# A linear-attention and mixture-of-experts kernel: the first own table and its gathers a step sooner, the second weight matrix loaded in the middle of the loop, other work moved between engines

## The chip, the cores and the metric

One core of one Trainium2 chip runs the whole program. The metric is the device time of one execution in microseconds (us); the kernel before took 648.4 us, the median of three runs (647.74 to 648.51).

## What is computed

A linear attention with decay gives `x`, 3072 rows of 512, and a layer of 8 experts with two experts per row follows. Cut from the reference:

```python
# attention, 4 batches, 8 heads, 768 positions, 64 wide, one decay gamma per head
state = gamma * state + einsum(k[t], v[t]);  y[t] = scale * einsum(q[t], state)
x = y.transpose(0, 2, 1, 3).reshape(3072, 512)
# experts
logits = x @ w_gate;  noisy = logits + log1p(exp(x @ w_noise)) * noise
top2 = two largest of noisy per row;  top2_w = softmax over the two
for e in range(8):  out[rows of e] += top2_w * (relu(x[rows of e] @ w1[e]) @ w2[e])
```

## The kernel before

**Stages.** The attention runs as a loop of 24 steps (`for j in range(NCH)`), one chunk of 128 positions each, 6 chunks per batch, from about 4 to 107 us. Behind the loop the first expert (number 0) begins, while the last chunk is still being routed; the eight experts then fill the rest of the span. All engines work through their instructions in the order in which the program writes them.

**One step j of the loop**, in the order written: `qk(j+1)` (TensorE, into PSUM tile `pA`), `x_turn(j-1)` (TensorE turns the scaled output `yt` back into rows and computes the gate products, into `pT`, of which there is one buffer), `y_state(j)` (TensorE, needs the state `U`), the entries of `middle` (TensorE pieces of the routing), `v_scale(j+1)` (GpSimd, gives `vp`), `masked(j+1)` twice (VectorE, frees `pA`), `x_scale(j-1)` (ScalarE squares `pT` and VectorE makes a power of two of the sum), the loads of chunk j+4 and the store of chunk j-2 on SyncE's DMA queue, `x_split(j-1)` (ScalarE reads `pT` at L411 and L425, makes the f16 high part at L426, and GpSimd the low part at L427), `y_mm(j)` (TensorE L373, then VectorE's `yt` at L377, then TensorE's state update L383 and ScalarE's copy `U` at L385), and last the entries that `P` (`mid`), `at` (`todo`) and `at0` (`first_todo`) have put into this step. So the VectorE entries of step j run while TensorE is already in step j+1.

**HALVES.** `x_turn(j)` uses 16 matmuls for a chunk in `HALVES` (even chunks below 16) and 32 half as wide ones for the others.

**Routing.** Chunks 0 to 11 are routing group 0, 12 to 17 group 1, 18 to 23 group 2: `route_x`, `route_b`, `route_t`, `route_i`, `route_m` (VectorE, with an Exp and an Ln on ScalarE), `route_p` (TensorE counts), `route_n`, `route_g` (gates), `route_d`. `gates_out` writes the gates to `xbuf` in HBM. For expert 0 the rows of group 0 are listed by `own_a`, `own_h`, `own_t`, `own_m`, `own_s`, `slots`; the first three blocks of 128 rows are then fetched by `gather` (GpSimd, an indirect DMA from `xbuf`) in steps 18 to 20 and turned by `x_t` (a DMA transpose on SyncE's queue, into `xe`) in steps 20 and 21.

**Weights.** `w_load` brings a quarter of a matrix (512 KB), `w_sum` squares it (ScalarE L210), `w_scale` (TensorE L220, VectorE) makes the scale, `w_hi` and `w_lo_half` the two f16 parts. w1 of expert 0 is loaded in steps 3 to 6, w2 in steps 20 and 21.

**Behind the loop**, in the order written: `gates_out(1)`, `route_d(1)`, `first(0)` (12 matmuls, L880 to L882, need `xe` of the first three blocks), `w_sum` of w2's last two quarters, four zero fills of the output, `x_store(22)`, `x_turn(23)`, `logits(23)`, `route_x(2)`, `x_scale(23)`, `x_last(23)`, `first(1)` with `w_scale` of w2 after its first six matmuls, `route_b/t/i/m(2)`, `first(2)`, `first(3)` with `route_p(2)` (L498, L500) after its first six matmuls, and so on.

Of the kernel before, what the change touches and what calls it, by code (L numbers as in the profile page):

```python
# [10 lines left out]
F32 = mybir.dt.float32  # L11
F16 = mybir.dt.float16
# [3 lines left out]
AF = mybir.ActivationFunctionType  # L16
OP = mybir.AluOpType
# [4 lines left out]
NC = S // C  # L22
NCH = B * NC
N = B * S
DM = H * D
# [35 lines left out]
SOON = _C["vtab"][1]  # L61
QW = HP * C + NC * HP
WARM, BUSY = (5, 2), 3
HALVES = range(0, 16, 2)


def _constants():
# [37 lines left out]
def moe_kernel(ctx, tc, qk_rows, vk_rows, noise, wgn, w1, w2, ctab, qtab, xbuf, out):  # L105
# [158 lines left out]
    def load(j, pairs=("qk", "vk")):  # L264
        for n in pairs:
            t = loads.tile([128, 2, DM], F32, name="in_" + n, bufs=AHEAD + 1)
            nc.sync.dma_start(t.rearrange("p a c -> p (a c)"), {"qk": qk_rows, "vk": vk_rows}[n][j])
            if n == "qk":
                IN["q", j], IN["k", j] = [t[:, i].rearrange("p (a c) -> p a c", a=HP) for i in range(2)]
            else:  # L270
                IN["v", j], IN["kt", j] = t[:, 0], t[:, 1]
# [47 lines left out]
        u = loads.tile([128, HP, D], F32, name=f"U{i}", bufs=1)  # L319
        U.append(u)  # L320

    VP, AM, PY, PT, YT, XS, X16, LG = {}, {}, {}, {}, {}, {}, {}, {}
    pctx = ExitStack()
    loop_psum = pctx.enter_context(tc.tile_pool(name="loop_psum", bufs=1, space=bass.MemoryType.PSUM))
    pU = psum.tile([128, 512], F32, name="pU")[:, :HP * 64].rearrange("p (a d) -> p a d", a=HP)
# [93 lines left out]
        nc.vector.tensor_scalar(XS[j].bitcast(I32), m[:, :1], -1.0, float((127 + TX + 62) << 23), op0=OP.mult, op1=OP.add)  # L419

    def x_split(j):
        X16[j] = x = work.tile([128, 2, DM], F16, name="x16", bufs=3)
        x32 = loads.tile([128, DM], F32, name="x32", bufs=2)
        logits(j)
        nc.scalar.activation(x32.rearrange("p (n x) -> p n x", x=64), PT.pop((j, "y")), AF.Copy, scale=XS[j])  # L425
        nc.scalar.activation(x[:, 0], x32, AF.Copy)  # L426
        nc.gpsimd.tensor_tensor(x[:, 1], x32, x[:, 0], op=OP.subtract)  # L427

    def x_last(j):
        X16[j] = x = work.tile([128, 2, DM], F16, name="x16", bufs=3)  # L430
# [87 lines left out]
        nc.vector.reciprocal(dn, dn)  # L518
        R[g] = (t2, den, dn)

    def route_g(g):

        t2, den, dn = R[g]
        sl, n = span(g), SPAN[g][1]
        nc.vector.tensor_tensor(ga[:, 0, sl], dn, invx[:, sl], op=OP.mult)
        nc.vector.tensor_tensor(ga[:, 1, sl], den, ga[:, 0, sl], op=OP.mult)
        t = temp([128, 2, n, NL], F32, "t", n)
        nc.vector.tensor_tensor(t, oh[:, :, sl], ga[:, :, sl, None].to_broadcast([128, 2, n, NL]), op=OP.mult)
        nc.vector.tensor_tensor(gateb[:, sl], t[:, 0], t[:, 1], op=OP.add)
        if g:  # L530
            nc.gpsimd.tensor_copy(gateb[:, sl, 0:1], gateb[:, sl, E:NL])

# [181 lines left out]
    def at(j, f, *a):  # L714
        todo.setdefault(j, []).append((f, a))
# [35 lines left out]
    def at0(j, f, *a):  # L751
        first_todo.setdefault(j, []).append((f, a))
# [3 lines left out]
    def P(j, f, *a, d=mid):  # L756
        d.setdefault(j, []).append((f, a))
# [5 lines left out]
    at0(12, route_x, 0, 6, 12)  # L763
    P(13, route_b, 0, 6, 12)
    P(13, route_t, 0, 6, 12)
    P(13, route_i, 0, 6, 8)
    P(14, route_i, 0, 8, 12)
    P(14, route_m, 0)
    at0(14, route_c, 0)
    P(15, route_p, 0, d=middle)  # L770
    P(15, route_n, 0)
    P(15, route_g, 0)
    P(16, route_d, 0)
    at(16, gates_out, 0)
    P(16, own_a, 0)
    P(16, own_h, 0, 0, 7)
    at(16, route_e, 0)
    P(17, own_h, 0, 7, 12)
    P(17, own_t, 0)
    P(18, own_m, 0, 0, 2 * NC, d=middle)  # L780
    P(18, own_s, 0)
    P(18, slots, 0, 3)
    for t in range(3):
        at(18 + t, gather, 0, t)
    P(20, x_t, 0, 0)
    P(21, x_t, 0, 1)
    at(21, x_t, 0, 2)
    at0(18, route_x, 1, 0, 6)
    P(20, route_b, 1, 0, 6)
    P(20, route_t, 1, 0, 6)  # L790
    P(21, route_i, 1, 0, 6)
    P(22, route_m, 1)
    at0(22, route_c, 1)
    P(23, route_p, 1, d=middle)
    P(23, route_n, 1)
    P(23, route_g, 1)
    at(3, turn_ident, 1)
    at(3, turn_gate, 1)
    at(1, nc.vector.memset, zero, 0.0)
    for i in range(4):  # L800
        at(3 + i, w_load, 0, "1", i)
        at0(5 + i, w_sum, 0, "1", i)
        at0((9, 9, 10, 11)[i], w_hi, 0, "1", i)
        at((20, 20, 21, 21)[i], w_load, 0, "2", i)
        if i < 2:
            at0(22 + i, w_sum, 0, "2", i)
    first_todo[9].insert(0, (w_scale, (0, "1")))
    for i, j in ((0, 10), (2, 10), (4, 11), (6, 12), (1, 18), (3, 19), (5, 19), (7, 21)):
        P(j, w_lo_half, 0, "1", i)
    at(3, nc.sync.dma_start, nz.rearrange("p c e -> p (c e)"), noise)  # L810
    at(4, nc.sync.dma_start, ct, ctab[:, SOON:])
# [16 lines left out]
    for j in range(NCH):  # L828
        more = j + 1 < NCH
        pA = qk(j + 1) if more else None  # L830
        if j:
            x_turn(j - 1)
        y_state(j)
        for f, a in middle.get(j, []):
            f(*a)
        if more:
            v_scale(j + 1)
        if more:
            masked(j + 1, pA, 0)
            masked(j + 1, pA, 1)  # L840
        if j:
            x_scale(j - 1)
        if j < NC - 3:
            q_table(j + 3)
        if j + AHEAD < NCH:
            load(j + AHEAD)
        if j > 1:
            x_store(j - 2)
        if j:
            x_split(j - 1)  # L850
        if j == 0:
            turn_gate(0)
        y_mm(j)
        for f, a in mid.get(j, []) + todo.get(j, []):
            f(*a)
        for f, a in first_todo.get(j, []):
            f(*a)
# [145 lines left out]
        return mm1_pe(0, 0, FIRST, f, between)  # L1003

    j = NCH - 1
    gates_out(1)
    route_d(1)
    p0 = first(0)
    for i in range(2, 4):
        w_sum(0, "2", i)  # L1010
    for i in range(4):
        zero_out(i)
    x_store(j - 1)
# [278 lines left out]
```

## Time and profile before

| what | value |
|---|---|
| median of three runs | 648.4 us |
| the profiled execution, its own time | 650.09 us |
| its span | 648.3 us |
| mean granted TensorE clock, as a share of full speed | 0.996 |
| TensorE matmul busy | 626.4 us (97%) |
| VectorE / ScalarE / GpSimd busy | 292.4 / 304.1 / 202.3 us |
| DMA | 113.05 MB, mean 174 GB/s |

A busy share is an average over stages. TensorE is the engine that is nearly always busy, so what counts is where it is not, what ends these waits, and where its steps in the loop are longer than the matmuls alone ask for.

### The profile page before, as it was taken

The numbers are of one execution on the slowest core, as the hardware profiler recorded it, in microseconds if no ns is written. First come the engines' busy times: TensorE is split into PE (matmuls) and PEld (weight loads), VectorE is DVE, ScalarE is ACT, GpSimd is POOL, SyncE is SP. The second block draws the span as 40 slices with busy tenths as digits, with TensorE's granted clock in tenths as the row PEclk, the third lists the DMA queues.
The fourth block names the chain that finished last, engine by engine and source line by source line (L and its number), as shares of the span: only waits on it lengthen the run. The fifth ranks groups of instructions, "written<-read, shape, count | busy, mean of one in ns | idle before, by whom it ended". The sixth has DMA issues, their size and how long they took to land.

```text
span 648.3 us, 12929 instructions
## 1 busy us (share of the span) xinstructions
PE 626.4 (97%) x5271; PEld 379.3 (59%) x5271; DVE 292.4 (45%) x743; ACT 304.1 (47%) x582; POOL 202.3 (31%) x165
## 2 busy tenths in 40 slices
PE   8999997799999999999999999999999999999995
PEld 5888885448668644554455445544554465445574
DVE  4677995698445222635163216321632172215020
ACT  5778455713653543443454345534553454344121
POOL 2545574031431044104330342034303430340214
PEclk9999998999999999999999999999999999999999
DMA  8999979998679066744775476547774775572303
GB/s 319 407 403 400 314 254 190 363 250 283 146 131 301 10 113 125 199 140 88 127 189 168 82 121 177 187 83 119 188 175 83 111 205 159 83 131 50 50 8 44
DMA packets 87513, 113.05 MB, mean 174 GB/s; under 512 B 59894, under 2 KB 61052, under 8 KB 83868
## 3 DMA queue, kind: packets, MB, share of 16 engines
q1 hardware_dynamic: 75664, 85.56, 43.7%
q0 software_dynamic: 11776, 26.63, 22.0%
q8 instruction: 42, 0.69, 0.4%
q14 instruction: 19, 0.16, 0.1%
q10 hardware_dynamic: 12, 0.01, 0.0%
HBM read 72.66 MB, written 26.42 MB: 153 GB/s over the span
## 4 chain that ended last, share of the span: by engine, by line
PE 87%; DVE 5%; DMA 3%; ACT 2%; issue 1%; POOL 1%; SPq 1%; POOLq 0%; ACTq 0%; DVEq 0%
PE pH L880 13%; PE pH L881 13%; PE pH L882 13%; PE pO L926 11%; PE pO L928 11%; PE pO L927 11%; PE pY L373 3%; PE pT L982 2%; PE pA L349 2%; PE pO L970 2%; PE pT L400 2%; DMA xg<-xbuf,idx 2%; DMA in_vk<-vk 1%; PE pY L366 1%; DMA wst<-w 1%
## 5 line engine op out<-in xcount | busy, mean ns | idle before, releaser
L880 PE MATMUL pH<-xe,w1h 128*128 128x384 f16 (+5 forms) x576 | 181.6, 315 | 3.5 <-DMA xe<-xg 2.8
L917 POOL DMA_INDIRECT out<-ot,idx x51 | 81.9, 1606 | 322.7 <-ACT ot L912 181.7
L881 PE MATMUL pH<-xe,w1h 128*128 128x384 f16 (+5 forms) x576 | 181.6, 315 | 0.0
L882 PE MATMUL pH<-xe,w1l 128*128 128x384 f16 (+5 forms) x576 | 181.5, 315 | 0.0
L889 DVE SCALAR_TENSOR_TENSOR hl<-pH,hh 128x384 f16<-128x384 f32 (+5 forms) x144 | 75.6, 527 | 139.8 <-ACT hh L886 139.1
L928 PE MATMUL pO<-w2h,hl 128*128 128x512 f16 x344 | 130.4, 379 | 0.0
L927 PE MATMUL pO<-w2l,hh 128*128 128x512 f16 x344 | 130.4, 379 | 0.0
L926 PE MATMUL pO<-w2h,hh 128*128 128x512 f16 x344 | 130.4, 379 | 0.0
L886 ACT ACTIVATE hh<-pH 128x384 f16<-128x384 f32 (+5 forms) x144 | 67.2, 468 | 122.6 <-PE pH L882 111.7
L912 ACT ACTIVATE ot<-pO,gse 128x512 f32<-128x512 f32 x45 | 30.9, 687 | 155.2 <-PE pO L928 142.9
L238 DVE SCALAR_TENSOR_TENSOR w1l<-wst,wsc,w1h 128x1024 f16<-128x1024 f32 x28 | 35.9, 1283 | 97.4 <-ACT w1h L233 97.4
L880 PEld LDWEIGHTS <-w1h 128*128 128x128 f16 x576 | 56.5, 98 | 37.4 <-issue 4.3
L882 PEld LDWEIGHTS <-w1l 128*128 128x128 f16 x576 | 56.5, 98 | 31.3 <-issue 0.5
L881 PEld LDWEIGHTS <-w1h 128*128 128x128 f16 x576 | 56.5, 98 | 31.0 <-issue 1.5
L210 ACT ACTIVATE junk<-wst 128x1024 bf16<-128x1024 f32 x64 | 67.2, 1050 | 4.9 <-DMA wst<-w 4.9
L729 POOL DMA_INDIRECT xg<-xbuf,idx x54 | 56.9, 1053 | 28.0 <-issue 13.3
L928 PEld LDWEIGHTS <-hl 128*128 128x128 f16 x344 | 33.7, 98 | 40.6
L926 PEld LDWEIGHTS <-hh 128*128 128x128 f16 x344 | 33.7, 98 | 40.5 <-issue 0.4
L927 PEld LDWEIGHTS <-hh 128*128 128x128 f16 x344 | 33.7, 98 | 39.6
L427 POOL TENSOR_TENSOR x<-x,x 128x512 f16<-128x512 f32 x23 | 28.7, 1249 | 40.5 <-ACT x L426 14.4
L233 ACT ACTIVATE w2h<-wst,wsc 128x1024 f16<-128x1024 f32 x32 | 36.5, 1140 | 0.6 <-DVE wsc L188 0.6
L233 ACT ACTIVATE w1h<-wst,wsc 128x1024 f16<-128x1024 f32 x32 | 36.1, 1137 | 0.0
(182 smaller groups left out, 656.1 us busy)
## 6 DMA issues: line engine op xcount, KB each, us to landing
wst<-w SPq DMA_DIRECT2D x28, 1024.0 KB, 5.3
in_qk<-qk SPq DMA_DIRECT2D x24, 512.0 KB, 5.2
in_vk<-vk SPq DMA_DIRECT2D x24, 512.0 KB, 7.8
xbuf<-x SPq DMA_DIRECT2D x24, 256.0 KB, 5.2
out<-zero SPq DMA_DIRECT2D x6, 1024.0 KB
wst<-w SPq DMA_DIRECT2D x8, 512.0 KB, 7.3
xg<-xbuf,idx POOLq DMA_INDIRECT x54, 4.4
xe<-xg SPq DMA_TRANSPOSE x54, 4.6
```

Of the source, the lines that this page charges most:

```text
L210: nc.scalar.activation(junk, st[:, i * 1024:(i + 1) * 1024], AF.Square, accum_out=ss[:, i:i + 1])
L233: nc.scalar.activation(hi, st[:, i * 1024:(i + 1) * 1024], AF.Copy, scale=sc[:, 0:1])
L729: nc.gpsimd.indirect_dma_start(out=x[:n], out_offset=None, in_=xbuf[:128 + B0 * S] if e == 0 and t < 3 else xbuf, in_offset=bass.IndirectO ...
L880: nc.tensor.matmul(p[:, :n], whi, xh, start=(k == 0), stop=False)
L881: nc.tensor.matmul(p[:, :n], whi, xl, start=False, stop=False)
L882: nc.tensor.matmul(p[:, :n], wlo, xh, start=False, stop=(k == KT - 1))
L886: nc.scalar.activation(hh[:, f, n0:n1], p, AF.Relu)
L889: nc.vector.scalar_tensor_tensor(hl[:, f, n0:n1], p, 0.0, hh[:, f, n0:n1], op0=OP.max, op1=OP.subtract)
L917: nc.gpsimd.indirect_dma_start(out=out, out_offset=bass.IndirectOffsetOnAxis(ap=idx[:n, i:i + 1], axis=0), in_=ot[:n], in_offset=None, com ...
L926: nc.tensor.matmul(p, a, WT["2h"][:, f, :], start=(f == 0), stop=False)
L927: nc.tensor.matmul(p, a, WT["2l"][:, f, :], start=False, stop=False)
L928: nc.tensor.matmul(p, c, WT["2h"][:, f, :], start=False, stop=(f == FT - 1))
```

## The change

The own table of expert 0 is made about a step earlier: all of `route_i(0)` in step 13, `route_d` and `own_a` in step 15, `own_h` in 15 and 16, `own_t` in 16, `own_m`, `own_s`, `slots` in 17; the gathers go to steps 17 to 19 and the transposes, each an entry of `mid` now, to 19 to 21. The two larger instructions of `route_g` (L528, L529) run on GpSimd for groups 0 and 1. Group 1's steps move one step forward, and `gates_out(1)` and `route_d(1)` go into steps 22 and 23. w2 of expert 0 is loaded in steps 14 to 17, one quarter each, and squared in steps 18, 20 and 22 and behind the loop. w1 is loaded from step 2 on, its `w_hi` goes to steps 10 to 13, one each, and its `w_lo_half` is spread anew. For chunks 0 to 5 and 8 (`DIRECT`) ScalarE writes the f16 high part straight from PSUM and VectorE makes the low part, from PSUM too; that low part, or for other chunks L426 and L427, now stands behind `y_mm`, so that the copy of `U` comes before them. `HALVES` gets 18, 20 and 22. The first load of v and k is two DMAs.

```diff
-HALVES = range(0, 16, 2)
+HALVES = [*range(0, 16, 2), 18, 20, 22]
+DIRECT = [0, 1, 2, 3, 4, 5, 8]
...
+            if n == "vk" and j == 0:
+                for i in range(2):
+                    nc.sync.dma_start(t[:, i], src[:, i * DM:(i + 1) * DM])
...
     def x_split(j):
-        x32 = loads.tile([128, DM], F32, name="x32", bufs=2)
+        X16[j] = work.tile([128, 2, DM], F16, name="x16", bufs=3), PT.pop((j, "y"))
         logits(j)
-        nc.scalar.activation(x32.rearrange("p (n x) -> p n x", x=64), PT.pop((j, "y")), AF.Copy, scale=XS[j])
-        nc.scalar.activation(x[:, 0], x32, AF.Copy)
-        nc.gpsimd.tensor_tensor(x[:, 1], x32, x[:, 0], op=OP.subtract)
+        x, py = X16[j]
+        if j in DIRECT:
+            nc.scalar.activation(x[:, 0].rearrange("p (n x) -> p n x", x=64), py, AF.Copy, scale=XS[j])
+        else:
+            X32[0] = loads.tile([128, DM], F32, name="x32", bufs=2)
+            nc.scalar.activation(X32[0].rearrange("p (n x) -> p n x", x=64), py, AF.Copy, scale=XS[j])
+
+    def x_low(j):
+        x, py = X16[j]
+        X16[j] = x
+        if j in DIRECT:
+            xv = [x[:, a].rearrange("p (n x) -> p n x", x=64) for a in range(2)]
+            nc.vector.scalar_tensor_tensor(xv[1], py, XS[j], xv[0], op0=OP.mult, op1=OP.subtract)
+        else:
+            nc.scalar.activation(x[:, 0], X32[0], AF.Copy)
+            nc.gpsimd.tensor_tensor(x[:, 1], X32[0], x[:, 0], op=OP.subtract)
...
-    def route_g(g):
+    def route_g(g, eng=nc.vector):
...
-        nc.vector.tensor_tensor(t, oh[:, :, sl], ga[:, :, sl, None].to_broadcast([128, 2, n, NL]), op=OP.mult)
-        nc.vector.tensor_tensor(gateb[:, sl], t[:, 0], t[:, 1], op=OP.add)
+        eng.tensor_tensor(t, oh[:, :, sl], ga[:, :, sl, None].to_broadcast([128, 2, n, NL]), op=OP.mult)
+        eng.tensor_tensor(gateb[:, sl], t[:, 0], t[:, 1], op=OP.add)
...
-    P(13, route_i, 0, 6, 8)
-    P(14, route_i, 0, 8, 12)
+    P(13, route_i, 0, 6, 12)
...
-    P(15, route_g, 0)
-    P(16, route_d, 0)
+    P(15, route_d, 0)
+    P(15, own_a, 0)
+    P(15, route_g, 0, nc.gpsimd)
+    P(15, own_h, 0, 0, 2)
     at(16, gates_out, 0)
-    P(16, own_a, 0)
-    P(16, own_h, 0, 0, 7)
-    at(16, route_e, 0)
-    P(17, own_h, 0, 7, 12)
-    P(17, own_t, 0)
-    P(18, own_m, 0, 0, 2 * NC, d=middle)
-    P(18, own_s, 0)
-    P(18, slots, 0, 3)
+    P(16, own_h, 0, 2, 12)
+    P(16, own_t, 0)
+    P(16, route_e, 0)
+    P(17, own_m, 0, 0, 2 * NC, d=middle)
+    P(17, own_s, 0)
+    P(17, slots, 0, 3)
     for t in range(3):
-        at(18 + t, gather, 0, t)
-    P(20, x_t, 0, 0)
-    P(21, x_t, 0, 1)
-    at(21, x_t, 0, 2)
+        at(17 + t, gather, 0, t)
+        P(19 + t, x_t, 0, t)
...
     for i in range(4):
-        at(3 + i, w_load, 0, "1", i)
-        at0(5 + i, w_sum, 0, "1", i)
-        at0((9, 9, 10, 11)[i], w_hi, 0, "1", i)
-        at((20, 20, 21, 21)[i], w_load, 0, "2", i)
-        if i < 2:
-            at0(22 + i, w_sum, 0, "2", i)
-    first_todo[9].insert(0, (w_scale, (0, "1")))
-    for i, j in ((0, 10), (2, 10), (4, 11), (6, 12), (1, 18), (3, 19), (5, 19), (7, 21)):
+        at(2 + i, w_load, 0, "1", i)
+        at0((5, 6, 8, 9)[i], w_sum, 0, "1", i)
+        at0(10 + i, w_hi, 0, "1", i)
+        at(14 + i, w_load, 0, "2", i)
+        if i < 3:
+            at0((18, 20, 22)[i], w_sum, 0, "2", i)
+    first_todo[10].insert(0, (w_scale, (0, "1")))
+    for i, j in ((0, 11), (1, 11), (2, 12), (3, 12), (4, 14), (5, 18), (6, 18), (7, 20)):
...
         y_mm(j)
+        if j:
+            x_low(j - 1)
...
-    gates_out(1)
-    route_d(1)
     p0 = first(0)
-    for i in range(2, 4):
-        w_sum(0, "2", i)
+    w_sum(0, "2", 3)
```

## Rows read from the trace of the kernel before

**Rows 1.** Windows: us, then each engine's busy time, granted clock, DMA share, GB/s.

```profile
11.42:27.00 15.58, 15.58 (x358) 14.22 (x354) 11.18 (x27) 10.75 (x31) 8.61 (x8) 1.00 1.03 409
...
72.73:89.44 16.71, 15.86 (x368) 13.64 (x365) 16.02 (x44) 8.64 (x23) 10.09 (x8) 1.00 0.87 285
89.44:107.20 17.76, 15.59 (x361) 13.06 (x359) 13.16 (x48) 11.70 (x31) 11.26 (x11) 1.00 0.92 195
107.20:123.24 16.04, 9.86 (x78) 5.22 (x77) 7.32 (x45) 8.57 (x19) 1.40 (x2) 0.89 0.93 302
123.24:160.00 36.76, 36.76 (x280) 23.64 (x280) 34.24 (x92) 11.04 (x21) 7.99 (x7) 1.00 0.87 270
```

**Rows 2.** Timeline of TensorE behind the loop: start, us, what, idle before and releaser.

```profile
109.98 0.40 PE L880 MATMUL pH<-xe,w1h 128*128 128x384 f16 x1 [2.77 <-DMA xe<-xg]
...
113.71 0.78 PE L400 MATMUL pT<-turn,yt 64*64 64x80 f32 x32
...
116.58 0.16 PE L220 MATMUL pR<-wsb,oneb 128*128 128x4 bf16 x1 [1.01 <-ACT wsb L216]
...
119.37 0.33 PE L882 MATMUL pH<-xe,w1l 128*128 128x384 f16 x1
...
123.24 0.18 PE L498 MATMUL pR<-mb,trib 128*128 128x54 bf16 x1 [1.65 <-DVE mb L487]
```

**Rows 3.** First gather (timeline), last gather (chain), the transposes that wait (timeline).

```profile
88.44 1.15 POOL L729 DMA_INDIRECT xg<-xbuf,idx  x1 [0.17 <-issue]
...
96.78 10.14 DMA xg<-xbuf,idx
...
97.56 11.09 SPq L747 DMA_TRANSPOSE xe<-xg  x2
```

**Rows 4.** Timeline of ScalarE behind the loop.

```profile
113.51 1.06 ACT L210 ACTIVATE junk<-wst 128x1024 bf16<-128x1024 f32 x1 [4.37 <-DMA wst<-w]
...
116.44 0.21 ACT L411 ACTIVATE lgs<-pT 128x64 f32<-128x64 f32 x1
```

**Rows 5.** Timeline of the loop's first step: GpSimd's first v_scale, TensorE's first y_mm.

```profile
8.84 1.04 POOL L330 TENSOR_TENSOR vp<-in_vk,cs 128x512 f32<-128x512 f32 x1 [7.77 <-DMA in_vk<-vk]
...
9.93 1.09 PE L373 MATMUL pY<-am,vp 128*64 128x128 f32 x16 [1.23 <-POOL vp L330]
```

**Rows 6.** Chain that ended last, undisturbed steps: start, us on the chain, what.

```profile
19.25 1.09 PE pA L349 x16
...
22.82 0.47 PE pU L383 x16
23.28 1.09 PE pA L349 x16
...
27.01 1.09 PE pA L349 x16
```

**Rows 7.** Timeline of TensorE: four waits inside the loop.

```profile
42.71 0.49 PE L373 MATMUL pY<-am,vp 128*64 128x128 f32 x5 [0.59 <-issue]
...
70.70 0.21 PE L498 MATMUL pR<-mb,trib 128*128 128x108 bf16 x1 [0.72 <-DVE mb L487]
...
76.86 1.75 PE L349 MATMUL pA<-in_qk 64*128 64x128 f32 x16 [0.33 <-DVE am L354]
...
104.70 0.71 PE L400 MATMUL pT<-turn,yt 64*64 64x80 f32 x28 [1.13 <-issue]
```

**Rows 8.** Timeline: VectorE's route_g, own_h, low part in x_last; the gates' DMA and landing.

```profile
73.94 1.23 DVE L528 TENSOR_TENSOR t<-oh,ga 128x216 f32<-128x216 f32 x1
...
82.48 0.82 DVE L571 TENSOR_TENSOR a<-lanes,lf 128x640 f16<-128x640 f16 x1
...
119.64 0.75 DVE L434 SCALAR_TENSOR_TENSOR x<-pT,xsa,x 128x512 f16<-128x512 f32 x1 [0.81 <-ACT x L433]
...
76.23 0.39 SPq L536 DMA_DIRECT2D xbuf<-gateb  x1
...
DMA to landing us min/median/max: 3.0/3.0/3.0
```

## What I predict

> **What bounds the kernel now.** I read the windows first, then TensorE's timeline behind the loop, then who ends its waits there, and last its waits inside the loop. The windows [rows 1] show three kinds of stretch. From 123.24 on TensorE is busy all the time (36.76 of 36.76 us), so whatever reaches that point sooner makes the end sooner by as much, as long as everything that follows moves with it. From 107.20 (the end of the last `y_mm`) to 123.24 it is busy for 9.86 of 16.04 us, and its granted clock is 0.89 of full speed: this is the gap. Inside the loop it is nearly always busy; an undisturbed step takes 4.03 us with the 16-matmul `x_turn` and 3.73 with the 32-matmul one, from one `qk` to the next [rows 6], and the later steps are longer. VectorE, 16.02 of 16.71 us busy between 72.73 and 89.44, is what TensorE waits for there.
>
> The gap has four parts [rows 2]. `first(0)` waits 2.77 us for `xe`. Its 12 matmuls then take 3.73 us (109.98 to 113.71), while 17 such matmuls behind the second wait take 2.79 (116.58 to 119.37), so 12 would take 1.95: after the wait they run at the lower of the two clock levels, 1.2 GHz. `w_scale` of w2 costs 1.01, `first(3)` then waits for `x_last`, and `route_p(2)` waits 1.65 for the routing of the last chunk. The releasers lead back to one place. The last gather took 10.14 us to land, beside the loads of w2, and the transposes on SyncE's queue waited for it (11.09 us with the two issues) [rows 3]; the second half of w2 stands behind them in that queue, so ScalarE waits 4.37 us for it, and `logits(23)`, behind the two sums in ScalarE's order, starts at 116.44 although its `x_turn` was done at 114.49 [rows 2, 4].
>
> **The change part by part. Behind the loop.** Gathers and transposes come a step sooner, without w2 in their way. A step is some 4 us, so the last gather goes out about 92.5; even if it took its 10.14 us again, it would be there at 102.6, before the loop's end. So I take the wait at 0, and the lower clock with it. What is late next: `first(0)` takes 1.95 us, `x_turn(23)` 0.78, and from `logits(23)` to `route_p(2)` the path takes 123.24 - 116.44 = 6.80 us, the way through `x_scale`, `x_last`, `route_b` to `route_m`, which the change leaves alone; its TensorE work in between (first(1), first(2), half of first(3), 4.9 us) is hidden by it. That gives 9.5 us. The other end: `w_sum` of the last quarter still stands before `logits(23)`, and the sum in step 22 is in front of it on ScalarE; with about 1.25 us each (1.06 [rows 4] and the readout, estimated) ScalarE can be up to 1 us late, so 10.5. I take 10.0, the middle, since ScalarE's two sums fall where it also makes the high part. 16.04 - 10.0 = **6.0 saved** (5.5 to 6.5). `gates_out(1)` and `route_d(1)` leave this place for steps where VectorE has little else; I count nothing for them, and under 0.5 if that cover fails.
>
> **v and k apart.** The first `y_mm` waits 1.23 us for `vp`, and that for the load [rows 5]. At 409 GB/s [rows 1] the 256 KB of k are 0.6 us. `qk(1)` lies in front of it on TensorE and leaves room. **0.6 saved** (0 if the halves land together, to 0.65).
>
> **The low part by VectorE.** In the seven steps behind the chunks in `DIRECT`, 0.75 us [rows 8] comes behind `yt` on VectorE, and the next `x_turn` now waits for it, since it reads the only `pT`. `yt` (estimated at 0.7 from the low part, which has its size) and the low part end some 1.65 us after `y_mm`, with a hop of about 0.1 each; TensorE has 0.47 + 1.09 = 1.56 us of its own in between [rows 6]. So the least is 0.1 a step, 0.7 in all; where VectorE is late anyway (it is 72% busy there, 11.18 of 15.58 [rows 1]) it is the whole 0.75, 5.3 in all. Near the lower end, with one late step and the chunk behind which TensorE has no `pU` to make, I take **1.5 lost**. The copy of `U` in front of the high part, and GpSimd's work that falls away, save nothing on TensorE there. `w_hi` one to a step instead of two takes a peak off ScalarE; I count nothing for it.
>
> **Steps 14 to 18.** Four `route_i` leave step 14, so `route_m` comes sooner and the 0.72 wait of `route_p(0)` can go; `route_g`'s 1.23 and its smaller companion leave VectorE [rows 8], and with them the 0.33 wait of `qk` at 76.86 and its stretch to 1.75 [rows 7] instead of 1.09 [rows 6]. That is 1.7 of gain. Against it, `own_h` for ten chunks and `own_t` now stand just before `own_m` of the next step: five chunks took 0.82 [rows 8], so with `own_t` some 2 us behind `yt`, about what TensorE has to do until `own_m`; if VectorE is a little late, TensorE waits up to 1. **1.0 saved** (0 to 1.7), nearer the gain, since the heavier of VectorE's instructions leave.
>
> A rule weighs on this. L528 took 1.23 us for 216 columns and the low part 0.75 for 512 [rows 8]: the row is long for its size. The Trainium skill, GPSIMD Engine Reference, section 8 (Key points), says that GpSimd shares its SBUF interfaces with VectorE, that instructions with two SBUF inputs contend, and that VectorE is about twice as fast at elementwise work. By that rule the move to GpSimd makes the work longer and holds up `own_a` and `own_h` beside it, and this part's 1.0 would be 0; the row shows the contention before the move already, so I keep 1.0.
>
> **Steps 19 to 23.** The wait of 1.13 us at 104.70 names no engine [rows 7]; it falls when w2 and the gather fill the DMA engines, which the change ends, so 1.1 saved (0 to 1.13). 18, 20 and 22 in `HALVES` cost 4.03 - 3.73 = 0.3 a step [rows 6], 0.9 lost (0 where the step waits for VectorE anyway). The sums of w2 in steps 18 and 20 put 1.25 us in front of ScalarE's next square, and `x_turn` waits for `pT` behind it: 0.4 lost (0 to 2.5). Group 1's entries come a step sooner, and the last step of the loop holds none of the heavy ones: 1.0 saved (0 to 2, since TensorE stands idle for 17.76 - 15.59 = 2.2 us there [rows 1], 1.1 of them counted already, and is slowed besides). **0.8 saved** (-2.3 to 3.1).
>
> **w2 in the loop.** Four loads of 512 KB are 2.1 MB, 5.1 us at 409 GB/s, in a stretch whose DMA share is 0.87 [rows 1]. The inputs are asked for three steps, some 12 us, ahead, so I see no wait for them. The nearest cost is the nameless wait of 0.59 at 42.71 [rows 7], from a stretch where w1 was just loaded; none to two such: **0.5 lost** (0 to 1.2).
>
> **The sum**: 6.0 + 0.6 - 1.5 + 1.0 + 0.8 - 0.5 = 6.4 us. The profiled execution took 650.09 us with a span of 648.3; it would be 643.7 and 641.9. The median of the runs, 648.4, lies at the span, so the forecast is 648.4 - 6.4 = **642.0**. Its own range is 640 to 644.5.
>
> **The rivals.** (a) *The loop gives back all that it waits for*: the low part hides wholly (0.7 lost), steps 14 to 23 give 1.7 + 2.5 and w2 costs nothing: 6.2 + 0.6 - 0.7 + 4.2 = 10.3, 638.1. For it speaks VectorE's load, against it that the change puts ScalarE's sums into the same steps. (b) *`xe` is late all the same*: gates or gathers are held up by w2's transfers, and `first(0)` still waits 1 to 2 us and then runs at the lower clock (1.8 more); of 6.4 some 3 remain, 645.3. For it speaks that the loads of w2 now end just where the gathers begin; against it the 4 us of room. (c) *Slower: the first gather blocks GpSimd.* It reads the gates that `gates_out(0)` writes, and behind it in GpSimd's order stands the `v_scale` of a chunk whose `y_mm` comes about a step later. The gates went out at 76.23 and landed in 3.0 us [rows 8]; the first gather was issued at 88.44 [rows 3], now at about 84. If the gates stand behind all of w2 (5.1 us), they land at about 85 and cost next to nothing. From about 87 on, when that `y_mm` is due, each further us is a us lost; beyond 93.4, 17 us after the issue, all 6.4 are gone, and at 96 the time is 651.0. For it speaks that the gates are 1536 short rows, against it the landing of 3.0 us in a loaded stretch. The Trainium skill, DMA: Bandwidth & Descriptors, Specifications, wants pieces of 512 bytes or more for full rate; no row here shows the gates' rate by itself. (d) *Nothing gained*: `DIRECT` costs its 5.3 and ScalarE's sums their 2.5: 6.4 - 3.8 - 2.1 = 0.5 left, 647.9.
>
> **How the numbers follow.** Chances: the forecast 0.62, (a) 0.12, (b) 0.14, (c) 0.07, (d) 0.05. The range takes in the forecast's own, (b) and half of (a): **638.0 to 646.0**. About 0.2% (1.3 us) is what a measurement of this kernel can tell from no change; forecast, (a) and (b) lie beyond that: faster 0.88, same 0.05, slower 0.07.
>
> **What would show it.** In the profile after: `first(0)` starts right behind the last `y_mm`, without a wait on `xe`, at a granted clock of 1.00 (if not, (b)); w2's last sum ends before or about when `x_turn(23)` does, `logits(23)` follows at once, and `route_p(2)` still waits for `mb`, with about 10.0 us from the loop's end to it. The loop's end lies at 106 to 107.5. `x_turn` in the first steps waits for L434's like on VectorE by 0.1 to 0.75. GpSimd's gather in step 17 does not hold its `v_scale` (if it does, (c)). The forecast is wrong if TensorE shows new idle time behind `route_p(2)`, where I moved everything together, or if the chain from `logits(23)` to `mb` is no longer 6.8 us.

## The result: slower by 1.2%

The changed kernel took 655.86 us, median of four runs (655.11 to 656.24); the kernel before took 648.43 beside it. The ratio is 1.0116, 95% interval 1.0098 to 1.0133. The prediction was 642.0, faster; it was wrong in sign. The profiled execution took 656.14 us, with a span of 654.3 and a mean granted clock of 0.990. The profiled execution of the kernel before (650.09) was 1.7 above its median, so the two traces show 6.0 of the 7.4 us between the medians.

The windows of the changed kernel (us, busy time of each engine, granted clock, DMA share, GB/s): an early stretch, one in the loop, the part behind the loop, the stretch after it up to 160 us.

```profile
11.42:27.00 15.58, 14.58 (x324) 12.98 (x320) 11.63 (x28) 7.97 (x25) 5.74 (x6) 1.00 1.02 407
...
93.58:108.18 14.60, 11.02 (x182) 9.68 (x178) 11.35 (x27) 6.71 (x17) 8.92 (x8) 0.78 0.81 279
...
119.56:129.21 9.65, 7.94 (x76) 4.61 (x76) 5.21 (x36) 6.83 (x15) 1.33 (x2) 1.00 0.88 312
129.21:160.00 30.79, 30.79 (x214) 18.21 (x214) 28.98 (x81) 9.08 (x16) 8.37 (x7) 1.00 0.87 253
```

Against [rows 1]: the part behind the loop is 9.65 us where it was 16.04, and from 129.21 on TensorE is busy all the time, as it was before from 123.24 on. But the loop ends at 119.56 instead of 107.20, and TensorE, which had no idle time in the early stretch, now has 1.0 us there. The timeline around the loop's end (start, us, what, idle before and releaser):

```profile
111.06 1.29 SPq L765 DMA_TRANSPOSE xe<-xg  x1
...
119.50 0.34 PE L899 MATMUL pH<-xe,w1h 128*128 128x384 f16 x1
...
121.55 0.78 PE L406 MATMUL pT<-turn,yt 64*64 64x80 f32 x32
...
122.40 0.23 ACT L417 ACTIVATE lgs<-pT 128x64 f32<-128x64 f32 x1 [0.20 <-PE pT L406]
...
129.21 0.18 PE L516 MATMUL pR<-mb,trib 128*128 128x54 bf16 x1 [1.65 <-DVE mb L505]
```

Beside [rows 2 to 4]: `first(0)` starts with no wait, the last transpose takes 1.29 where two took 11.09, and from `logits(23)` to `route_p(2)` it is 6.81 us as it was 6.80. So the part behind the loop gained and the whole loss lies in the loop. This table gives it in stretches, each from one `qk` to another on TensorE's timeline, each row from one profiled execution (`qk(k)` is the first TensorE work of step k - 1; LE is the end of the last `y_mm`; us):

| kernel | to qk(8) | 8 to 13 | 13 to 16 | 16 to 20 | 20 to 22 | 22 to LE | LE to `route_p(2)` | sum |
|---|---|---|---|---|---|---|---|---|
| before | 34.5 | 21.5 | 11.4 | 18.3 | 8.7 | 12.8 | 16.0 | 123.2 |
| changed | 37.4 | 21.4 | 16.6 | 18.2 | 14.6 | 11.3 | 9.7 | 129.2 |
| changed, halves apart | 37.2 | 21.3 | 12.8 | 18.2 | 9.5 | 11.4 | 9.7 | 120.1 |
| changed, halves from PSUM | 37.1 | 21.6 | 15.2 | 18.2 | 9.5 | 11.3 | 9.7 | 122.6 |
| changed, old w1 schedule | 36.4 | 21.5 | 11.2 | 18.2 | 12.7 | 12.0 | 9.7 | 121.7 |
| changed, old low part | 35.2 | 21.2 | 16.2 | 18.6 | 14.5 | 11.4 | 9.7 | 126.7 |
| changed, both | 34.5 | 21.7 | 12.9 | 18.2 | 10.1 | 14.0 | 9.7 | 121.1 |
| changed, w2 late | 36.2 | 21.7 | 14.9 | 19.8 | 8.7 | 11.3 | 11.7 | 124.4 |
| before, w2 early | 34.5 | 21.5 | 11.4 | 18.2 | 10.0 | 11.7 | 10.0 | 117.3 |
| before, new w1 schedule | 34.2 | 21.3 | 16.9 | 17.4 | 11.0 | 13.3 | 14.4 | 128.5 |

The changed kernel loses 2.9 us before qk(8), 5.2 from qk(13) to qk(16) and 5.9 from qk(20) to qk(22). Two lines of the list of what ends TensorE's waits in the loop (us in total, times, longest); between them stand smaller waits for ScalarE and waits that name no engine:

```profile
PE pA L355 <- DVE am L360: 4.4, 3, 2.7
...
PE pT L406 <- DVE x L442: 1.6, 4, 0.6
```

The last line is the low part in the early steps. The first is `masked`, VectorE's work that frees `pA`. What made it late is in the timeline of VectorE and GpSimd in steps 11 and 12, then in step 18:

```profile
59.22 1.17 POOL L445 TENSOR_TENSOR x<-x,x 128x512 f16<-128x512 f32 x1 [1.50 <-DMA in_vk<-vk]
59.50 2.88 DVE L246 SCALAR_TENSOR_TENSOR w1l<-wst,wsc,w1h 128x512 f16<-128x512 f32 x2
60.33 1.50 POOL L336 TENSOR_TENSOR vp<-in_vk,cs 128x512 f32<-128x512 f32 x1
62.30 1.28 DVE L360 TENSOR_TENSOR am<-pA,mask 128x512 f32<-128x512 f32 x2
...
65.48 1.29 POOL L445 TENSOR_TENSOR x<-x,x 128x512 f16<-128x512 f32 x1 [3.64 <-DMA in_qk<-qk]
65.66 1.31 DVE L465 TENSOR_TENSOR lgs<-lgs 128x192 f32<-128x192 f32 x1
66.72 1.15 POOL L336 TENSOR_TENSOR vp<-in_vk,cs 128x512 f32<-128x512 f32 x1
67.01 0.98 DVE L466 TENSOR_TENSOR lg<-lgs 128x96 f32<-128x96 f32 x1
...
71.36 1.34 PE L406 MATMUL pT<-turn,yt 64*64 64x80 f32 x32 [0.96 <-ACT x L435]
...
93.33 1.15 POOL L747 DMA_INDIRECT xg<-xbuf,idx  x1 [0.17 <-DVE xsa L425]
93.86 3.83 DVE L246 SCALAR_TENSOR_TENSOR w1l<-wst,wsc,w1h 128x512 f16<-128x512 f32 x2
94.52 1.05 POOL L336 TENSOR_TENSOR vp<-in_vk,cs 128x512 f32<-128x512 f32 x1
95.68 1.46 POOL L445 TENSOR_TENSOR x<-x,x 128x512 f16<-128x512 f32 x1
97.30 1.25 POOL L747 DMA_INDIRECT xg<-xbuf,idx  x1 [0.15 <-issue]
97.61 0.35 DVE L465 TENSOR_TENSOR lgs<-lgs 128x192 f32<-128x192 f32 x1
98.00 1.75 DVE L466 TENSOR_TENSOR lg<-lgs 128x96 f32<-128x96 f32 x1
98.57 1.05 POOL L336 TENSOR_TENSOR vp<-in_vk,cs 128x512 f32<-128x512 f32 x1
...
100.40 2.10 PE L355 MATMUL pA<-in_qk 64*128 64x128 f32 x16 [2.71 <-DVE am L360]
```

Two halves of w1 (L246) take 2.88 us in step 11 and 3.83 in step 18. In the kernel before, two of them took 1.41 where GpSimd stood still (its L245, the same instruction):

```profile
90.80 1.41 DVE L245 SCALAR_TENSOR_TENSOR w1l<-wst,wsc,w1h 128x512 f16<-128x512 f32 x2
92.12 1.28 DVE L354 TENSOR_TENSOR am<-pA,mask 128x512 f32<-128x512 f32 x2
92.15 1.15 POOL L427 TENSOR_TENSOR x<-x,x 128x512 f16<-128x512 f32 x1 [1.47 <-issue]
```

So the rows suggest this **theory**: a VectorE instruction with two inputs in SBUF and a GpSimd instruction shut each other out; one waits while the other runs. The halves, `route_x` (L465, L466) and others read two SBUF tiles. `masked` (L360) reads PSUM and one SBUF tile, and keeps its 1.28 us for two. The change puts two halves each into steps 11, 12 and 18, of which 12 and 18 also hold `route_x`; such a row of instructions no longer fits before GpSimd's two, and then waits for one or more of them at each meeting. In step 12 it is not the two halves that stretch (1.41 us) but the two instructions of `route_x` behind them (1.31 and 0.98, against 0.35 and 0.26 where nothing meets them). `masked` comes late, and TensorE waits. The Trainium skill, SBUF — State Buffer, section "SBUF: two separate sides", has such a rule: VectorE and GpSimd share one port pair under an exclusive lock, held for the whole instruction. The rivals: w2's transfers in the loop, other parts of w1's schedule, or simply too much VectorE work in these steps.

The clock adds to the waits. In the loop of the kernel before it is granted at 1.00; here it is 0.50, the lower of the two levels (1.2 GHz), in two stretches that begin at or just behind TensorE's waits (of 0.78 and 0.96 us, and of 2.71):

```profile
70.94:74.35 3.41, 2.99 (x56) 2.66 (x58) 3.27 (x26) 2.89 (x7) 2.12 (x2) 0.50 0.23 90
101.66:108.49 6.83, 6.07 (x90) 5.32 (x88) 4.33 (x24) 3.71 (x11) 3.20 (x3) 0.50 0.58 141
```

At 0.50 an `x_turn` takes 1.34 us, at 1.00 it takes 0.78. By that ratio the 9.06 us of TensorE work in these stretches cost nearly 4 us more than at full clock (an estimate): about a third of what the loop lost.

### The profile page after: what moved, and what is told of

It is laid out like the page before. It is cut to its first block, busy times and chain, and to the rows that moved or that the text cites. A ratio compares the mean times of both kernels' runs of the same rounds, so it can differ in the third digit from the quotient of the medians.

```text
span 654.3 us, 12825 instructions
## 1 busy us (share of the span) xinstructions
PE 632.3 (97%) x5223; PEld 384.9 (59%) x5223; DVE 300.9 (46%) x746; ACT 299.8 (46%) x575; POOL 196.4 (30%) x162
## 4 chain that ended last, share of the span: by engine, by line
PE 87%; DVE 6%; ACT 3%; DMA 2%; issue 1%; POOL 0%; POOLq 0%; ACTq 0%; DVEq 0%; SPq 0%
PE pH L899 13%; PE pH L901 13%; PE pH L900 13%; PE pO L945 11%; PE pO L947 11%; PE pO L946 11%; PE pT L406 2%; PE pY L379 2%; PE pT L1001 2%; PE pA L355 2%; PE pO L989 2%; DVE w1l L246 1%; DMA xbuf<-x 1%; PE pY L372 1%; DMA in_qk<-qk 1%; DVE am L360 1%
## 5 line engine op out<-in xcount | busy, mean ns | idle before, releaser
L936 POOL DMA_INDIRECT out<-ot,idx x51 | 84.2, 1650 | 321.7 <-ACT ot L931 192.3
L747 POOL DMA_INDIRECT xg<-xbuf,idx x54 | 55.1, 1021 | 28.8 <-DVE idx L660 12.0
L355 PE MATMUL pA<-in_qk 64*128 64x128 f32 x384 | 31.8, 298 | 5.0 <-DVE am L360 4.4
L234 ACT ACTIVATE w1h<-wst,wsc 128x1024 f16<-128x1024 f32 x32 | 36.2, 1137 | 0.0
```

The costliest lines, as they stand in the source:

```text
L234: nc.scalar.activation(hi, st[:, i * 1024:(i + 1) * 1024], AF.Copy, scale=sc[:, 0:1])
L747: nc.gpsimd.indirect_dma_start(out=x[:n], out_offset=None, in_=xbuf[:128 + B0 * S] if e == 0 and t < 3 else xbuf, in_offset=bass.IndirectO ...
L936: nc.gpsimd.indirect_dma_start(out=out, out_offset=bass.IndirectOffsetOnAxis(ap=idx[:n, i:i + 1], axis=0), in_=ot[:n], in_offset=None, com ...
```

## The experiments

"Before" was 648.8 to 649.5 us in the runs beside these; ratios are to it.

**One part of the change put back.** w1's schedule as before the change:

```diff
-        at(2 + i, w_load, 0, "1", i)
-        at0((5, 6, 8, 9)[i], w_sum, 0, "1", i)
-        at0(10 + i, w_hi, 0, "1", i)
+        at(3 + i, w_load, 0, "1", i)
+        at0(5 + i, w_sum, 0, "1", i)
+        at0((9, 9, 10, 11)[i], w_hi, 0, "1", i)
...
-    for i, j in ((0, 11), (1, 11), (2, 12), (3, 12), (4, 14), (5, 18), (6, 18), (7, 20)):
+    for i, j in ((0, 10), (2, 10), (4, 11), (6, 12), (1, 18), (3, 19), (5, 19), (7, 21)):
```

> The changed kernel with only w1's schedule put back (loads in steps 3 to 6, w_hi in 9, 9, 10, 11, w_lo_half of eight halves in 10, 10, 11, 12, 18, 19, 19, 21). Theory L (VectorE's instructions with two SBUF inputs wait for GpSimd's: in the changed kernel the halves in pairs in steps 12 and 18 took 2.88 and 3.83 us instead of 1.41): the losses around 59 to 68 and 93 to 105 us go, 6 to 8 of the loop's 12.3, so 648 to 650. Theory M (w2's transfers in steps 14 to 17 are the cause): no change, 655 to 656.5. Theory N (the low part, its order and VectorE's share of it, is the cause): no change, 655 to 656.5.

Measured 649.01, ratio 0.9998 (0.9983 to 1.0013): 6.9 us come back, as the theory had it, and qk(13) to qk(16) is 11.2 again. Next, `DIRECT` empty and the low part in its old place, ahead of `y_mm`:

```diff
-DIRECT = [0, 1, 2, 3, 4, 5, 8]
+DIRECT = []
```

> The changed kernel with the low part as before (high part from x32, low part by GpSimd, in x_split, ahead of y_mm, for all chunks). Theory L: the 2.3 us lost up to 31 us go, the collisions of the pairs of halves stay: 652 to 654. Theory M: 652 to 654 as well. Theory N: GpSimd's subtraction comes 0.4 us sooner against VectorE's entries again, and most of the 12.3 goes: 643 to 647.

Measured 653.04, 1.0038 (1.0000 to 1.0075): 2.8 back by the medians, though the five runs go from 648.29 to 654.21. The profiled execution has 2.2 of it in the stretch to qk(8), and the losses at qk(13) and qk(20) stay. Then w2 back in steps 20 and 21:

```diff
-        at(14 + i, w_load, 0, "2", i)
+        at((20, 20, 21, 21)[i], w_load, 0, "2", i)
```

> The changed kernel with w2 loaded in steps 20 and 21 again, its sums in 22, 23 and behind the loop. Theory L: the loop's loss stays within 2 us, and behind the loop 1 to 4 us of the gain are lost again: 656 to 659. Theory M: the loop's loss goes, 646 to 650. Theory N: as L.

Measured 654.86, 1.0087 (1.0060 to 1.0114), 1.0 below the changed kernel, which no theory had said: in the profiled execution the loop is 6.9 us shorter (it ends at 112.66), the part behind it 2 us longer; the profiled span is 3.3 us shorter, of which the median shows only 1.0 (the seven runs go from 652.12 to 657.28). That kept open whether w2's transfers cost the loop something.

**One part alone, in the kernel before.** Only w2 in steps 14 to 17, squared in 18, 20, 22 and behind the loop:

> The kernel before with one part of the change: w2 loaded in steps 14 to 17, squared in 18, 20, 22 and behind the loop. Theory L and N: the loop as before within 1.5 us (ScalarE's sums), the last gather lands in some 5 us, first(0) waits no more, from the loop's end to route_p(2) about 10 us instead of 16: 642 to 645. Theory M: the loop 5 us longer or more, 648 or more.

Measured 645.47, 0.9937 (0.9914 to 0.9961), the clearest gain, and 0.5 above the range expected. Its TensorE rows behind the loop:

```profile
107.23 0.34 PE L880 MATMUL pH<-xe,w1h 128*128 128x384 f16 x1
...
117.29 0.19 PE L498 MATMUL pR<-mb,trib 128*128 128x54 bf16 x1 [1.65 <-DVE mb L487]
```

The loop ends at 107.30 (107.20 before), and `route_p(2)` follows 10.0 us later: w2 alone gives the 6.0 us behind the loop, without earlier gathers, and its transfers cost the loop nothing that the trace shows. Behind `route_p(2)` this execution takes 1.3 us more than the kernel before (526.35 us to the end of the span, 525.07 before), 0.7 of it in a wait of TensorE for VectorE (L880 for L889) that was not there. Only w1's new schedule:

> The kernel before with one part of the change: w1's schedule (loads from step 2, w_hi in 10 to 13, w_lo_half in 11, 11, 12, 12, 14, 18, 18, 20). Theory L: the pairs of halves meet GpSimd here too, their mean rises from 0.74 to over 1.0 us, the loop gets 2 to 6 us longer: 650 to 655. If the pairs only hurt together with the moved own table: within 1 us of 649.

Measured 654.73, 1.0074 (1.0050 to 1.0098): most of the loss, without any other part of the change; qk(13) to qk(16) takes 16.9. The earlier own table (own steps, gathers and group 1 a step sooner, `route_g` on GpSimd), on top of w2 early:

> The kernel before with w2 loaded early, and the own table, gathers, transposes and group 1 a step sooner with route_g on GpSimd, w1's schedule and the low part as before. Beside w2 early alone (645.5): if the own table's move is free, 644 to 646; by the trace of the changed kernel with the old w1 schedule (own_m waits 1.2 us, qk 2.5 us for VectorE) it costs 2 to 4 us: 647.5 to 650.

Measured 646.93, 0.9971 (0.9949 to 0.9993): between the two expectations, and no better than w2 early. Its profiled execution (648.98, one of the slower of ten that go from 645.18 to 651.41) ended the loop at 112.2, with 3.8 us in two waits of TensorE that name no engine; what these are stays open. Squares of w2 in other steps:

```diff
+        at0((16, 17, 19, 21)[i], w_sum, 0, "2", i)
```

> The kernel before with w2 loaded in steps 14 to 17, and squared in steps 16, 17, 19 and 21, where ScalarE has room, and none behind the loop. With the sums in 18, 20, 22 TensorE's step 20 took 6.2 us instead of 5.0; that goes, and w_scale behind the loop needs no sum: 1 to 1.5 us better than 645.5, so 644 to 645. If the sums' place doesn't matter: 645 to 646.

Measured 645.71, 0.9941 (0.9920 to 0.9963): no difference to the first place, as the second of the two expectations had it. The low part alone (`DIRECT` and its new place):

> The kernel before, with only the low part changed: DIRECT for chunks 0 to 5 and 8, VectorE making their low part from PSUM, and the low part placed behind y_mm for all chunks. My prediction's term: 1.5 us lost (0.7 to 5.3), so 650 to 651. Theory: the same sign, +1 to +3 against the kernel before, as waits of x_turn for VectorE in steps 2 to 6; the low part reads PSUM and one SBUF tile, so it does not stretch beside GpSimd. Rival (GpSimd's lighter load makes it a gain): 1 us faster.

Measured 650.84, 1.0030 (1.0011 to 1.0049): 1.9 lost. The profiled execution, the fastest of the ten (649.38), reaches qk(8) 1.5 us later and still ends the loop at 107.22, so it does not show where the 1.9 of the median lie. v and k apart and the three `HALVES`, on w2 early:

> The kernel before, with w2 loaded in steps 14 to 17 and squared in 18, 20, 22 and behind the loop, and two small parts of the change added: the first load of v and k as two DMAs, and 18, 20 and 22 in HALVES. My prediction's terms: 0.6 saved and 0 to 0.9 lost against w2 early alone (645.5), so 644.9 to 645.8. Theory from the changed kernel's trace: v and k apart save nothing, HALVES costs 0 to 0.9: 645.5 to 646.4.

Measured 645.89, 0.9937 (0.9912 to 0.9962), not to be told from w2 early alone.

**The disputed mechanism by itself.** In front of the loop, scratch instructions of the size of a half: VectorE's with two SBUF inputs, then beside GpSimd's subtraction, then with one PSUM and one SBUF input, then casts with one SBUF input:

```diff
+    def two(o):
+        nc.vector.scalar_tensor_tensor(lo_[:, o, :512], zero, gt[:, 0:1], hi_[:, 0, :512], op0=OP.mult, op1=OP.subtract)
+    def one(o):
+        nc.vector.scalar_tensor_tensor(lo_[:, o, :512], t[:, 0], gt[:, 0:1], hi_[:, 0, :512], op0=OP.mult, op1=OP.subtract)
+    def pool(f):
+        nc.gpsimd.tensor_tensor(gl_[:, 0, :], zero, lo_[:, f, :512], op=OP.subtract)
```

> A probe: the kernel before with some 40 extra instructions in front of the loop (scratch data; the time of the whole isn't used). VectorE and GpSimd alone and beside each other: the 128x512 form of w_lo (two inputs from SBUF), the low part's form (one input from PSUM, one from SBUF), and a cast with one SBUF input; GpSimd's subtraction, four at a time. Theory L: the form with two SBUF inputs takes about 0.74 us alone and about 1.9 beside GpSimd (it waits for a whole GpSimd instruction of 1.17), GpSimd's grows alike; the form with one PSUM input stays at 0.75. Rival: VectorE's rows stay at 0.74 in all cases, and the long ones of the changed kernel have another cause.

The groups of instructions of one execution (form, count, busy us, mean ns): VectorE alone, then beside GpSimd, then with the PSUM input beside GpSimd:

```profile
L835 DVE SCALAR_TENSOR_TENSOR w1l<-zero,gt,w1h 128x512 f16<-128x512 f32 x4 | 3.0, 756 | 0.1
...
L844 POOL TENSOR_TENSOR w2h<-zero,w1l 128x512 f16<-128x512 f32 x4 | 6.0, 1508 | 3.2 <-DVE w1l L835 3.0
L835 DVE SCALAR_TENSOR_TENSOR w1l<-zero,gt,w1h 128x512 f16<-128x512 f32 x4 | 5.3, 1329 | 0.1
...
L844 POOL TENSOR_TENSOR w2h<-zero,w1l 128x512 f16<-128x512 f32 x3 | 3.5, 1154 | 0.6 <-DVE w1l L854 0.4
L838 DVE SCALAR_TENSOR_TENSOR w1l<-pT,gt,w1h 128x512 f16<-128x512 f32 x4 | 3.0, 748 | 0.1
```

The casts on the timeline; the first one starts ahead of GpSimd's first instruction, the other three meet it:

```profile
31.57 0.42 DVE L841 CAST w1l<-zero 128x512 f16<-128x512 f32 x1
...
32.02 3.84 DVE L841 CAST w1l<-zero 128x512 f16<-128x512 f32 x3
...
33.08 3.80 POOL L863 TENSOR_TENSOR w2h<-zero,w1l 128x512 f16<-128x512 f32 x3
```

With two SBUF inputs it is 0.76 alone and 1.33 on the mean beside GpSimd: the one that started ahead of GpSimd's kept 0.75, each of the other three took 1.52. GpSimd's own instruction goes from 1.15 to 1.51. With a PSUM input it is 0.75 beside GpSimd, which keeps its 1.15. A cast with one SBUF input takes 0.42 where it starts first, and 1.26 in each of the three meetings. The lock of the Trainium skill's page fits in kind, and so does its condition (two SBUF inputs, or a faster mode that uses both ports). In size it is a little milder, and below the 1.9 expected: the pairs follow each other 1.56 us apart, where it would be 0.76 + 1.15 = 1.91 if each had to wait for the whole of the other.

**The mechanism in the changed kernel.** First the halves in other steps, none beside `route_x`, nothing else touched:

```diff
-    for i, j in ((0, 11), (1, 11), (2, 12), (3, 12), (4, 14), (5, 18), (6, 18), (7, 20)):
+    for i, j in ((0, 11), (1, 11), (2, 14), (3, 19), (4, 20), (5, 21), (6, 21), (7, 22)):
```

> The changed kernel, with only the places of w1's halves in the loop altered: chunks of w1 at steps 11, 11, 14, 19, 20, 21, 21, 22, so that no half stands in the steps 12 and 18 that also hold route_x. The loads, squares, w_scale and w_hi of w1 stay where the change puts them. Theory (VectorE's instructions with two SBUF inputs and GpSimd's shut each other out, and trains of them cost steps): most of the 6.9 us that w1's old schedule gave back come back, 649 to 651. Rival (the other parts of w1's schedule, its earlier loads and w_hi one to a step, cost the time): 654 to 657.

Measured 646.60, 0.9953 (0.9935 to 0.9970): 9.3 us come back, more than expected, from six places in one line. From 8 us to the loop's end the granted clock is 1.00 here, so the stretches at the lower clock went with the waits. In step 12 `route_x` is short again:

```profile
64.11 0.35 DVE L465 TENSOR_TENSOR lgs<-lgs 128x192 f32<-128x192 f32 x1
...
64.49 0.26 DVE L466 TENSOR_TENSOR lg<-lgs 128x96 f32<-128x96 f32 x1
64.67 1.28 DVE L360 TENSOR_TENSOR am<-pA,mask 128x512 f32<-128x512 f32 x2
```

But moving work away would also help if VectorE merely had too much to do there. So the halves stay, and only their first input moves out of SBUF:

```diff
+        if (e, which) == (0, "1"):
+            src = pR[:, 511:512].to_broadcast([128, 512])
```

> The changed kernel, with the eight halves of w1 of expert 0 left in their steps, but their first input is one column of PSUM repeated 512 times in place of the loaded weight in SBUF. So the low part of that one weight matrix is left out of the computation; VectorE has the same number of instructions of 512 columns in the same places, but they read one SBUF input and one PSUM input. Theory (mutual exclusion: the halves cost because they read two SBUF inputs beside GpSimd): each half takes about 0.75 us on VectorE instead of 1.23, and most of the 9 us that placing them apart gave back come back with nothing moved: 647 to 651. Rival (steps 11, 12 and 18 simply hold too much VectorE work, and an instruction of 0.75 us costs the same from wherever it reads): 653 to 657.

Measured 648.94, 0.9994 (0.9968 to 1.0019): 6.9 us come back with the same instructions in the same steps. The group of the eight halves, in the changed kernel, and then in this one:

```profile
L246 DVE SCALAR_TENSOR_TENSOR w1l<-wst,wsc,w1h 128x512 f16<-128x512 f32 x8 | 9.6, 1229 | 0.0
```

```profile
L249 DVE SCALAR_TENSOR_TENSOR w1l<-pR,wsc,w1h 128x512 f16<-128x512 f32 x8 | 5.7, 741 | 0.0
```

So the lock, not the amount of work, carries most of it. qk(20) to qk(22) falls to 9.5, all that moving them gave. From qk(13) to qk(16) only 1.4 of 3.8 come back. There the short halves still push `route_x` into GpSimd's pair, and the clock still falls to 0.50 from 69.95 to 73.36:

```profile
63.92 1.16 POOL L449 TENSOR_TENSOR x<-x,x 128x512 f16<-128x512 f32 x1 [2.89 <-ACT x L448]
64.10 1.19 DVE L469 TENSOR_TENSOR lgs<-lgs 128x192 f32<-128x192 f32 x1
65.03 1.16 POOL L340 TENSOR_TENSOR vp<-in_vk,cs 128x512 f32<-128x512 f32 x1
65.33 0.98 DVE L470 TENSOR_TENSOR lg<-lgs 128x96 f32<-128x96 f32 x1
```

In that stretch the amount of work decides too, by where it puts the next two-input instruction.

The length of the halves alone does not decide, though. With the old w1 schedule put back the eight take 1.18 us on the mean, hardly less than the 1.23 of the changed kernel, and that kernel is 6.9 us faster. What the trace shows beside it is that `masked` is late less often: TensorE waits 4.4 us for it in the changed kernel and 2.5 with the old schedule.

**Do the losses add, and does w2 cost the loop?** Halves apart and the old low part together; then halves apart and w2 back in steps 20 and 21:

> The changed kernel with both costly parts taken out: w1's halves at steps 11, 11, 14, 19, 20, 21, 21, 22, and the low part made as before the change. Theory (two separate losses that add): 646.6 less the 2.8 us that the low part cost in the changed kernel, 643.8 (643 to 645), and the first gap behind the loop stays at about 10 us. Rival (the low part's loss was only time that the next late step would have cost anyway, so the two don't add): 646 to 647.5.

Measured 647.60, 0.9973 (0.9951 to 0.9995): not below 646.60, so the two don't add, as the rival said (0.1 above its range). In the profiled executions the 2.7 us won before qk(8) are given back at the end (22 to LE: 14.0 instead of 11.4), in waits for VectorE:

```profile
102.28 1.75 PE L355 MATMUL pA<-in_qk 64*128 64x128 f32 x16 [0.73 <-DVE am L360]
108.68 1.12 PE L406 MATMUL pT<-turn,yt 64*128 64x80 f32 x16 [1.42 <-DVE cb L532]
```

> The changed kernel with w1's halves at steps 11, 11, 14, 19, 20, 21, 21, 22, and w2 loaded in steps 20 and 21 again. It tells why putting w2 back made the changed kernel's loop 6.9 us shorter. Theory (w2's transfers cost the loop little; they only set the times so that halves, route_x and GpSimd met): the loop shortens by 0 to 2 and the part behind it grows by about 2: 646.5 to 649. Rival (w2's transfers themselves cost the loop about 6): 641 to 644.

Measured 650.21, 1.0018 (0.9993 to 1.0043), 3.6 above the same kernel with w2 early (646.60). In the profiled executions the loop ends at 109.74 instead of 110.39, so w2 costs it 0.65 at most, and the part behind grows by 2.2 to 11.9. Another 1.3 lies behind `route_p(2)`, where the granted clock is 0.50 from 121.11 to 124.52. The 6.9 us by which late w2 had shortened the changed loop were therefore not w2's transfers themselves. The trace of that run shows the meetings shifted: the two halves of step 18 take 1.79 us there instead of 3.83, and the `qk` behind them waits 0.31 for `masked` instead of 2.71. Why they shifted is not shown.

**A better version**: the kernel before with w2 early, squares in steps 16, 17, 19, 21, and one half moved from step 18 to 22.

> The kernel before, with w2 loaded in steps 14 to 17, its squares in steps 16, 17, 19 and 21, and the half of chunk 1 of w1 moved from step 18, where it stands beside route_x, to step 22. Theory: one meeting of two-input instructions with GpSimd less, so 0.5 to 1 us better than w2's squares alone (645.7): 644.5 to 645.5. Rival (VectorE is late in step 22 as well, or the step was not late): 645.5 to 647.

Measured 645.18, 0.9946 (0.9928 to 0.9964): faster than both kernels, and not to be told from w2 early alone (645.47). The half in step 18 cost nothing that can be measured.

## Why the prediction was wrong, point by point

- **What bounds the kernel**: right. What reached `route_p(2)` later made the end later by as much: it comes 5.97 us later, and the span grew by 6.0.
- **Behind the loop, 6.0 saved (5.5 to 6.5)**: right; 16.04 - 9.65 = 6.4 in the changed kernel, 6.0 with w2 early alone, at the granted clock of 1.00. But w2 alone does nearly all of it. The gathers did not even come sooner: I had put the last one at about 92.5, and it went out at 105.44, since the loop itself was late; it was in time because the loop's end had moved as well.
- **v and k apart, 0.6 saved**: nothing. The first `y_mm` starts at 9.96 us, 9.93 before [rows 5]; the added runs show nothing either. I had 0 as the bound.
- **The low part, 1.5 lost (0.7 to 5.3)**: right in sign and kind. The stretch to qk(8) is 2.9 longer in the changed kernel; made alone, the low part cost 1.9 in the whole time. I had counted one late step; the waits for L442 come in four, 1.6 us in all, 0.33 and 0.57 among them:

```profile
17.34 0.78 PE L406 MATMUL pT<-turn,yt 64*64 64x80 f32 x32 [0.33 <-DVE x L442]
21.71 1.12 PE L406 MATMUL pT<-turn,yt 64*128 64x80 f32 x16 [0.57 <-DVE x L442]
```

- **Steps 14 to 18, 1.0 saved**: nothing in steps 15 to 18 (qk(16) to qk(20): 18.3 before, 18.2 after); step 14 lies in the stretch that the halves spoiled. `route_p(0)`'s wait of 0.72 went, but `own_m` now waits for VectorE, 0.6 in the changed kernel and 2.0 with the halves apart. The rule of the Trainium skill that I had cited gave 0, which is what was measured, though the gain and the new wait that make up this 0 were not measured singly. I kept 1.0 because "the row shows the contention before the move already". That row, L528 with 1.23 us, was the lock at work: in the run with the low part alone the same instruction started ahead of GpSimd's and took 0.38.

```profile
75.00 0.38 DVE L541 TENSOR_TENSOR t<-oh,ga 128x216 f32<-128x216 f32 x1
```

  I read the 1.23 as the price of one instruction instead of a rule for all of them.
- **Steps 19 to 23, 0.8 saved**: 0.7 once the halves are apart (20 to 22 loses 0.7, 22 to LE gains 1.4). The terms that make it up were not measured singly, so the fit may be luck.
- **w2 in the loop, 0.5 lost**: 0.1 with w2 early alone, inside the range.
- **The step that failed** is one that has no number. Of w1 I wrote of `w_hi` alone, "I count nothing for it", and of the halves, "spread anew" in the section on the change, nothing at all. Each is 0.74 us of VectorE, and I took its duration, and that of `route_x` behind it, as belonging to the instruction. It belongs to the place as well: 1.41 for two halves when GpSimd stands still, 2.88 or 3.83 beside it. The new places cost 9.3 us against places apart, 6.9 of them by having both inputs in SBUF, and 6.9 against the old schedule; both numbers hold the waits and the lower clock together. With the halves apart the changed kernel is at 646.60, 4.6 above the forecast, with the kernel before 0.6 higher beside it. The rest is mostly the 2.7 instead of 1.5 to qk(8), 1.4 in qk(13) to qk(16), where two halves still stand in step 11 and `qk` waits 0.9 for `masked`, and the terms of 0.6 and 1.0 that came to nothing.
- **The rivals**: none was this one. The slower rival (c), a blocked first gather, did not happen: it waits 0.17 us, and for VectorE. (a), (b) and (d) didn't either. The chance of 0.07 for slower held only mishaps that I had seen in the rows of what the change names; the row for a VectorE step in full, where one more instruction meets GpSimd, I had not looked for.

## What to carry to other kernels

An instruction that is moved is costed at its new place: for each VectorE instruction with two SBUF inputs, look in the timeline which GpSimd instructions run there, and add for each that it meets (0.77 us a meeting in the probe; 1.5 for L466 here), and look what stands behind it in VectorE's order. A row that is long for its size is a sign of a rule that works on every instruction of that kind, so look for the others before going on. Losses in such a loop don't add, since a step that comes sooner meets other work; change one part at a time, and keep the part that pays (here w2 alone). After a wait, look at the granted clock as well: part of the loss was there.

## What the runs showed of the hardware

I had not expected how much one SBUF input more decides: the same VectorE instruction beside the same subtraction takes 1.52 us with two inputs in SBUF and 0.75 with one of them in PSUM. Nor that a cast with a single SBUF input is hit hardest, 0.42 to 1.26. Whether the issue of an indirect DMA by GpSimd counts as a meeting stays open. In step 18 two halves took 3.83 us with a gather's issue, a `v_scale` and a subtraction in a row on GpSimd. But `route_x`'s first instruction took its usual 0.35 in the middle of the next gather's issue (97.61, the issue from 97.30 to 98.55); the second, which started 0.4 later in the same issue with a `v_scale` behind it, took 1.75. In the kernel before, that second instruction took its usual 0.26 wholly beside a gather's issue (at 88.53). That was not tried by itself.
